# An FNet block with a feed-forward layer, in split float32 products: roots by GpSimd's power, first tiles of x rounded from x, the norms of the second half at other places

## The chip, the cores and the metric

The kernel runs on one core of a Trainium2 chip. A core has five engines, each with its own queue of instructions that it works through in order: TensorE (PE in the profile, with its weight loads as PEld), VectorE (DVE), ScalarE (ACT), GpSimd (POOL) and SyncE (SP), which here only issues transfers. The metric is the time of one execution on the device, in microseconds (us). The profile is one execution, recorded instruction by instruction; its span runs from the first to the last recorded instruction.

## The reference

```python
def reference(A_x, A_dft_seq_re, A_dft_seq_im, A_dft_hid_re, A_dft_hid_im, B_x, B_w1, B_w2):
    ...
        a = jnp.einsum("bsd,ed->bse", x, dft_hid_re)
        b = jnp.einsum("bsd,ed->bse", x, dft_hid_im)
        y = jnp.einsum("ts,bse->bte", dft_seq_re, a) - jnp.einsum("ts,bse->bte", dft_seq_im, b)
    ...
        h = jnp.einsum("bsd,df->bsf", x, w1)
        h = _silu(h)
        out = jnp.einsum("bsf,fd->bsd", h, w2)
    ...
    x = A_x
    h = x + _A_ref(_layernorm(x, axis=-1), A_dft_seq_re, A_dft_seq_im, A_dft_hid_re, A_dft_hid_im)
    h2 = h + _B_ref(_layernorm(h, axis=-1), B_w1, B_w2)
    return h2
```

x has 2048 rows of 512 columns, the hidden width is 1792, everything is float32. Both layer norms need the root 1 / sqrt(variance + 1e-5): one per row.

## The kernel before

**Split products.** Each float32 operand is split in two parts: a high part, rounded by ScalarE to a format that TensorE takes at full rate, and the remainder, subtracted by DVE. `three` (lines 108 to 112) multiplies high by high, high by remainder and remainder by high, so there are three matmuls for each product of a 128 x 128 and a 128 x 512 block. `rounded` (lines 74 to 85) makes the two parts of a page; in the profile they are `ph` (ACT, line 77) and `pl` (DVE, line 81). Many products are saved with a seven-product scheme (`fast`, `up`, `down_fast`), for which DVE makes sums and differences first.

**Stages.** Of the sequence, the even blocks of 512 positions are half q = 0 and the odd ones q = 1. The order of stages is `plain(0, 0)` (cosine part for half 0: 16 steps of 24 matmuls over four groups jj of four row tiles of x), `fast(1, 0)`, `mix(0)` (hidden transform and the sum with x, giving h), `fast(0, 1)`, `fast(1, 1)`, `mix(1)`, then `up(0)`, `down(0)`, `up(1)` and `down_fast(1)` for the feed-forward layer.

**Order.** Nothing is scheduled by a tool: `step(n, mm, before, after)` advances a clock by n matmuls of 0.2265 us, and puts work of other engines into a list of events at times relative to it (`before`: so many us ahead of the step; `after`: behind its end). At the end of the kernel the events are sorted by time and emitted, and ORDERED engines (PE, DVE, ACT, GpSimd) keep that order. The transfers on SP follow as they are emitted. So an event's time decides only where an instruction stands in its engine's queue; when it runs is decided by what it waits for.

**The head.** `begin` (line 230) issues the loads of the first two tiles of x and of the first two pages of the cosine matrix. For each of the two tiles `begin_x` (line 246) runs: `stats_x` (mean and variance per row, DVE lines 148 and 149), `roots_x` (line 152), then ScalarE rounds the page of the matrix and `norm_x` (line 160) writes the normalised tile `xc` (line 166) and from it the two high parts `X` (line 177); the remainders come from `rest` on DVE (line 183). The third and fourth tile (jj 0, k 1) follow in one go, events at lines 274 to 276. For jj 1 to 3 the four tiles' statistics go together into one call of `roots_x` with four columns (line 291).

**The root.** `rsqrt(v, t, r, q)` (lines 92 to 106), all on DVE: a first guess from the bits of v (lines 94, 95), the half of v (line 98), and three Newton steps, each of three instructions on more than one column and of two on one column.

**The norm of h** is `norm_h(q, tau, start)` (line 474), called four times. Its parts stand at fixed distances from `start`: load h again from memory (-8), column sums over the 512 values, which lie across partitions: two sums on DVE and an all-reduce over partitions on GpSimd (`total`, line 466; 0), subtract the mean (7, 9), squares on ScalarE (10, 12), the same sums and all-reduce for the variance (15), its 512 numbers through memory into a tile of 128 x 4 (22), the root on DVE and its way through memory to all partitions (31), and the products (45, 47). The transfers of h to memory and of these small tiles are issued by GpSimd too.

**The up projection**, `up(q, lead, between)` (line 600): for each of seven pairs p of column blocks, seven products n of six matmuls each, in the order 1, 2, 3, 6, 4, 7, 5 with 3 and 4 belonging to the pair before. They go into two tiles of PSUM, `y` and `vx`; DVE adds (line 624) and ScalarE copies and takes silu (lines 621 to 638). PSUM holds four such tiles, so the tiles of a pair are those of the pair two before, and a product waits for the adds that still read them.

```python
        for d, f in ((-8, load), (0, mean), (7, lambda: center(0)), (9, lambda: center(1)),
                     (10, lambda: square(0)), (12, lambda: square(1)), (15, var), (22, once),
                     (31, root), (45, lambda: scale(0)), (47, lambda: scale(1))):
            at(start + d, f)
```

```python
    second = down(0), down_fast(1)
    norm_h(1, 0, clock[0] + 8)
    norm_h(1, 1, clock[0] + 36)
    up(0, 28, lambda: next(second[0]))
```

Of the kernel before, what the change touches and what calls it, by code (L numbers as in the profile page):

```python
# [7 lines left out]
F32 = mybir.dt.float32  # L8
# [30 lines left out]
def fnet_ffn_kernel(  # L39
# [52 lines left out]
    def rsqrt(v, t, r, q):  # L92

        nc.vector.tensor_scalar(t.bitcast(I32), v.bitcast(I32), 1, None, op0=ALU.logical_shift_right)
        nc.vector.tensor_scalar(
            r.bitcast(I32), t.bitcast(I32), -1.0, float(0x5F3759DF), op0=ALU.mult, op1=ALU.add
        )
        nc.vector.tensor_scalar(v, v, -0.5, None, op0=ALU.mult)
        for a, b in ((r, q), (q, r), (r, q)):
            if a.shape[-1] == 1:  # L100
                nc.vector.scalar_tensor_tensor(t, a, v, a, op0=ALU.mult, op1=ALU.mult)
# [3 lines left out]
            nc.vector.scalar_tensor_tensor(b, t, 1.5, a, op0=ALU.add, op1=ALU.mult)  # L105
        return q
# [19 lines left out]
    def at(t, f):  # L126
        events.append((t, 1, len(events), f))
# [13 lines left out]
    def stats_x(jj, which):  # L141

        if jj not in stats:
            stats[jj] = [], small.tile([P, 4, 2], F32, name="mv1"), small.tile([P, 5, 4], F32, name="rs1")
        done, mv, _ = stats[jj]
        for k, a in which:
            st = small.tile([P, 6], F32, name="st1")
            nc.vector.bn_stats(st, xraw[jj, k][:, a, :])
            nc.vector.bn_aggr(mv[:, len(done), :], st)
            done.append((k, a))  # L150

    def roots_x(jj):
        done, mv, w = stats.pop(jj)
        n = len(done)
        nc.vector.tensor_scalar(w[:, 0, :n], mv[:, :n, 1], EPS, None, op0=ALU.add)
        r = rsqrt(*(w[:, m, :n] for m in range(4)))
        nc.vector.scalar_tensor_tensor(w[:, 4, :n], mv[:, :n, 0], -1.0, r, op0=ALU.mult, op1=ALU.mult)
        return {t: (w[:, 4, j : j + 1], r[:, j : j + 1]) for j, t in enumerate(done)}

    def norm_x(jj, which, factors):  # L160

        for k, a in which:
            if (jj, k) not in xc:
                xc[jj, k] = page(f"xc{jj}{k}")
            bias, scale = factors[k, a]
            nc.scalar.activation(xc[jj, k][:, a, :], xraw[jj, k][:, a, :], AF.Identity, bias=bias, scale=scale)
        todo = []
        for k in sorted({k for k, _ in which}):
# [4 lines left out]
            for i in range(2):  # L173
                if (i, k, jj) not in X:
                    X[i, k, jj] = page(f"X{i}{k}{jj}", F32R, (2, 2, 256))
                t, src = X[i, k, jj], xc[jj, k][:, b, i * 256 : (i + 1) * 256]
                nc.scalar.activation(t[:, 0, b], src, AF.Copy)  # L177
                todo.append((t[:, 1, b], src, t[:, 0, b]))
        return todo
# [66 lines left out]
    def begin_x(key, a):  # L246
        stats_x(0, [(0, a)])
        late["x", a] = begin_half(key, a) + norm_x(0, [(0, a)], roots_x(0))

    def plain(c, q):  # L250


        def mul(jj, k, tau, tiles, parts):
# [4 lines left out]
            for a in tiles:  # L258
                for i in range(2):
                    w = X[i, k, jj]  # L260
                    for m in range(2):
                        d = slice(m * P, (m + 1) * P)
                        three(acc[c, q, i, tau][:, m, :], w[:, 0, a, d], w[:, 1, a, d], hi[:, a, :], lo[:, a, :],
                              jj == 0 and k == 0 and a == 0, jj == NJ - 1 and k == 1 and a == 1)
# [3 lines left out]
        for a in range(2):  # L268
            at(-98 + 4 * a, lambda a=a: begin_x(keys[0], a))
            at(-97 + 4 * a, lambda a=a: rest(late.pop(("x", a))))  # L270
# [4 lines left out]
        at(clock[0] - 6, lambda: early("x0", lambda: norm_x(0, [(1, 0), (1, 1)], late.pop("r0"))))  # L275
        at(clock[0] - 4, lambda: rest(late.pop("x0")))
        for jj, k, tau in [(jj, k, tau) for jj in range(NJ) for k in range(2) for tau in range(2)][2:]:
# [4 lines left out]
            if k == 0 and tau == 0:  # L282
# [8 lines left out]
                before.append((15 - 5 * (jj == 1), lambda jj=jj: early(("r", jj), lambda: roots_x(jj))))  # L291
            if jj == NJ - 1 and k == 1:
# [181 lines left out]
    def norm_h(q, tau, start):  # L474
# [26 lines left out]
        def once():  # L501
            nc.gpsimd.dma_start(token[0], ln.pop("v")[0:1, 1, :])
            ln["w"] = small.tile([P, 4, 4], F32, name="rs2")
            nc.gpsimd.dma_start(ln["w"][:, 0, :], token[0].rearrange("(p j) -> p j", j=4))

        def root():
            w = ln.pop("w")
            nc.vector.tensor_scalar(w[:, 0, :], w[:, 0, :], 1.0 / D, EPS, op0=ALU.mult, op1=ALU.add)
            r = rsqrt(*(w[:, n, :] for n in range(4)))
            nc.gpsimd.dma_start(token[1].rearrange("(p j) -> p j", j=4), r)  # L510
# [352 lines left out]
    norm_h(1, 0, clock[0] + 8)  # L863
    norm_h(1, 1, clock[0] + 36)
# [6 lines left out]
    nc.vector.memset(warm, 0.0)  # L871
    nc.scalar.activation(small.tile([P, 1], F32, name="table"), warm[:, :1], AF.Silu)
# [49 lines left out]
```

## Time and profile before

| | us |
|---|---|
| median of 3 runs | 703.69 |
| the three runs | 703.64, 703.69, 704.99 |
| the profiled execution | 704.96 |
| its span | 703.2 |
| TensorE busy in it | 689.8 |
| DVE busy | 525.6 |
| ACT busy | 320.1 |
| GpSimd busy | 72.2 |

The page of the profile gives busy times and 40 slices of the span; the views of the trace give waits (who waited for whom), the instructions in order of time, and the chain of work that ended last, followed back from the end. A row of the timeline reads: start, duration, engine, line, operation, what it writes <- what it reads with the shapes, how many of them, and in square brackets how long the engine was idle before it and what ended that. The matmuls of the profile overlap, so that a step of 0.227 us from one start to the next is full rate, though each of them shows 0.39. Names such as `raw`, `ph`, `xc` are those of the code without their numbers. Instructions that only set up, wait or issue are not counted as busy.

### The profile page before, as it was taken

The page shows a single profiled execution, that of the slowest core. Times are in us where ns is not written, and L with a number is a line of the kernel's source. Part 1 is how long each engine was busy: PE and PEld are TensorE (multiplying, and loading weights), DVE is VectorE, ACT ScalarE, POOL GpSimd, SP SyncE. Part 2 cuts the span into 40 slices and gives each one's busy share as a digit, 9 for nine tenths or more (in the row PEclk, how much of TensorE's full clock was granted, in tenths as well). Part 3 has the DMA queues.
Part 4 walks back from the last instruction along what each step waited for, and adds up shares of the span by engine and source line. Part 5 has one row for each costly group of instructions (what it writes and reads, how often), then busy time and mean ns, then how long its engine had stood idle before and what let it go on. Part 6 is the DMA issues. An engine that isn't in the chain of part 4 may idle for free.

```text
span 703.2 us, 8359 instructions
## 1 busy us (share of the span) xinstructions
PE 689.8 (98%) x3009; PEld 565.4 (80%) x3009; DVE 525.6 (75%) x702; ACT 320.1 (46%) x398; POOL 72.2 (10%) x90
## 2 busy tenths in 40 slices
PE   8899999999999999999999999997999999999996
PEld 5688888888888888888888888886888888888885
DVE  6699965997867799799979746597888143249975
ACT  4555564444333644444363226565464044565420
POOL 0000020000013200022000003332320000000000
PEclk9999999999999999999999999999999999999999
DMA  9715359557779868687795664315997096368432
GB/s 324 277 57 180 114 206 382 196 203 239 231 233 377 339 217 311 246 298 280 271 330 181 194 232 153 103 46 209 372 411 309 10 337 229 120 245 294 135 135 89
DMA packets 54137, 160.22 MB, mean 228 GB/s; under 512 B 5968, under 2 KB 13136, under 8 KB 54096
## 3 DMA queue, kind: packets, MB, share of 16 engines
q1 hardware_dynamic: 44464, 126.11, 51.3%
q0 software_dynamic: 9632, 33.58, 12.2%
q8 instruction: 23, 0.38, 0.2%
q14 instruction: 18, 0.15, 0.1%
HBM read 122.95 MB, written 36.72 MB: 227 GB/s over the span
## 4 chain that ended last, share of the span: by engine, by line
PE 91%; DVE 4%; ACT 2%; issue 1%; DMA 0%; ACTq 0%; DVEq 0%
PE m L110 11%; PE m L111 11%; PE m L112 11%; PE y L110 7%; PE y L111 7%; PE y L112 7%; PE c L110 4%; PE c L111 4%; PE c L112 4%; PE o L110 4%; PE o L112 4%; PE o L111 4%; PE f L110 3%; PE f L112 3%; PE f L111 3%; PE vx L110 2%
## 5 line engine op out<-in xcount | busy, mean ns | idle before, releaser
L77 ACT ACTIVATE ph<-raw 128x1024 fp32r<-128x1024 f32 x98 | 101.8, 1058 | 98.1 <-DVE raw L356 62.2
L81 DVE TENSOR_TENSOR pl<-raw,ph 128x1024 fp32r<-128x1024 f32 x98 | 122.5, 1261 | 25.4 <-ACT ph L77 11.3
L110 PE MATMUL m<-ph,S 128*128 128x512 f32 x192 | 74.7, 389 | 0.0
L111 PE MATMUL m<-pl,S 128*128 128x512 f32 x192 | 74.7, 389 | 0.0
L112 PE MATMUL m<-ph,S 128*128 128x512 f32 x192 | 74.7, 389 | 0.0
L356 DVE TENSOR_TENSOR raw<-raw,raw 128x1024 f32<-128x1024 f32 x48 | 60.6, 1262 | 4.0 <-DMA raw<-in_seq 4.0
L110 PE MATMUL m<-ph,X 128*128 128x512 f32 x144 | 56.0, 389 | 0.0
L111 PE MATMUL m<-pl,X 128*128 128x512 f32 x144 | 56.0, 389 | 0.0
L112 PE MATMUL m<-ph,X 128*128 128x512 f32 x144 | 56.0, 389 | 0.0
L110 PE MATMUL c<-ph,X 128*128 128x512 f32 x128 | 50.0, 397 | 3.1 <-ACT X L177 3.1
L111 PE MATMUL c<-pl,X 128*128 128x512 f32 x128 | 50.1, 395 | 0.0
L112 PE MATMUL c<-ph,X 128*128 128x512 f32 x128 | 50.0, 395 | 0.0
L624 DVE TENSOR_TENSOR g<-vx,cp 128x512 f32<-128x512 f32 x28 | 19.2, 689 | 38.8 <-PE vx L112 30.9
L112 PEld LDWEIGHTS m<-ph,S 128*128 128x128 f32 x192 | 36.0, 188 | 7.5
L110 PEld LDWEIGHTS m<-ph,S 128*128 128x128 f32 x192 | 36.0, 188 | 7.5
L111 PEld LDWEIGHTS m<-pl,S 128*128 128x128 f32 x192 | 36.0, 188 | 7.4
L621 ACT ACTIVATE g<-g 128x512 f32<-128x512 f32 x42 | 26.4, 628 | 22.4 <-DVE g L624 22.4
L110 PE MATMUL o<-ph,Uh 128*128 128x512 f32 x84 | 33.5, 399 | 2.1 <-ACT g L621 2.1
L110 PE MATMUL f<-gth,wf 128*128 128x512 f32 x84 | 32.9, 392 | 0.8 <-DVE r L789 0.8
L112 PE MATMUL o<-ph,Ul 128*128 128x512 f32 x84 | 33.3, 397 | 0.0
L111 PE MATMUL o<-pl,Uh 128*128 128x512 f32 x84 | 33.3, 396 | 0.0
L111 PE MATMUL f<-gtl,wf 128*128 128x512 f32 x84 | 32.7, 389 | 0.0
(260 smaller groups left out, 1554.2 us busy)
## 6 DMA issues: line engine op xcount, KB each, us to landing
raw<-in_seq SPq DMA_DIRECT2D x98, 512.0 KB, 5.8
sf<-sd SPq DMA_DIRECT2D x28, 512.0 KB, 6.6
wf<-wd SPq DMA_DIRECT2D x28, 512.0 KB, 4.7
w<-in_ffn SPq DMA_DIRECT2D x28, 256.0 KB, 4.7
hid<-in_hid SPq DMA_DIRECT2D x8, 512.0 KB, 4.5
c<-cd SPq DMA_DIRECT2D x8, 512.0 KB, 4.6
h<-in_xT SPq DMA_DIRECT2D x8, 512.0 KB, 5.7
hd<-h POOLq DMA_DIRECT2D x8, 512.0 KB, 6.9
```

The lines of the kernel that those rows point to most:

```text
L77: nc.scalar.activation(hi, src, AF.Copy, scale=sign)
L81: nc.vector.tensor_tensor(lo, src, hi, op=ALU.subtract)
L110: nc.tensor.matmul(acc, wh, mh, start=first, stop=False, skip_group_check=on)
L111: nc.tensor.matmul(acc, wh, ml, start=False, stop=False, skip_group_check=on)
L112: nc.tensor.matmul(acc, wl, mh, start=False, stop=last, skip_group_check=on)
L356: nc.vector.tensor_tensor(o, a, b, op=ALU.subtract)
L621: nc.scalar.activation(g[q, f][:, tau, :], src, AF.Silu)
L624: nc.vector.tensor_tensor(g[q, f][:, tau, :], src, other, op=ALU.add)
```

## The change

1. `rsqrt` no longer computes the guess and three Newton steps on DVE. GpSimd raises v to the power -0.5 (exponents in a small tile `power`, filled once), and one Newton step on DVE refines the result. The Newton step is a function of its own, called later: in `norm_h` 1.5 us behind in the order (`spread`, with the transfers that follow), for jj 1 to 3 of x 2 us (1.5 for jj 1) behind, and in the head behind the remainder of the first page.
2. The tiles of group jj 0 are normalised with `direct=True`: ScalarE writes the two high parts straight from x with the norm's scale and bias, tile by tile, then `xc`; the remainders are still `xc` less the high part.
3. In `mul` of `plain`, the steps with jj 0 and tau 0 issue for each tile first the eight products with the high part of X, then the four with its remainder.
4. `norm_h(1, 0)` starts at -4 in place of 8 and `norm_h(1, 1)` at 16 in place of 36, from the end of `mix(1)`.

```diff
@@ -89,21 +89,22 @@
-    def rsqrt(v, t, r, q):
-
-        nc.vector.tensor_scalar(t.bitcast(I32), v.bitcast(I32), 1, None, op0=ALU.logical_shift_right)
-        nc.vector.tensor_scalar(
-            r.bitcast(I32), t.bitcast(I32), -1.0, float(0x5F3759DF), op0=ALU.mult, op1=ALU.add
-        )
-        nc.vector.tensor_scalar(v, v, -0.5, None, op0=ALU.mult)
-        for a, b in ((r, q), (q, r), (r, q)):
-            if a.shape[-1] == 1:
-                nc.vector.scalar_tensor_tensor(t, a, v, a, op0=ALU.mult, op1=ALU.mult)
+    power = keep.tile([P, 4], F32, name="power")
+
+    def rsqrt(v, t, q):
+
+        nc.gpsimd.tensor_tensor(q, v, power[:, : q.shape[-1]], op=ALU.pow)
+        nc.vector.tensor_scalar(t, v, -0.5, None, op0=ALU.mult)
+
+        def refine():
+            if q.shape[-1] == 1:
+                nc.vector.scalar_tensor_tensor(t, q, t, q, op0=ALU.mult, op1=ALU.mult)
             else:
-                nc.vector.tensor_tensor(t, a, a, op=ALU.mult)
+                nc.vector.tensor_tensor(v, q, q, op=ALU.mult)
                 nc.vector.tensor_tensor(t, t, v, op=ALU.mult)
-            nc.vector.scalar_tensor_tensor(b, t, 1.5, a, op0=ALU.add, op1=ALU.mult)
-        return q
+            nc.vector.scalar_tensor_tensor(q, t, 1.5, q, op0=ALU.add, op1=ALU.mult)
+
+        return refine
...
     def roots_x(jj):
+
         done, mv, w = stats.pop(jj)
         n = len(done)
...
+        v, t, r, b = (w[:, m, :n] for m in range(4))
+        nc.vector.tensor_scalar(v, mv[:, :n, 1], EPS, None, op0=ALU.add)
+        refine = rsqrt(v, t, r)
+
+        def then():
+            refine()
+            nc.vector.scalar_tensor_tensor(b, mv[:, :n, 0], -1.0, r, op0=ALU.mult, op1=ALU.mult)
+            return {x: (b[:, j : j + 1], r[:, j : j + 1]) for j, x in enumerate(done)}
+
+        return then
...
+        for k, a in which if direct else ():
+            for i in range(2):
+                put(X[i, k, jj][:, 0, a], k, a, slice(i * 256, (i + 1) * 256))
+            put(xc[jj, k][:, a, :], k, a, slice(0, 512))
+            todo += [(X[i, k, jj][:, 1, a], xc[jj, k][:, a, i * 256 : (i + 1) * 256], X[i, k, jj][:, 0, a]) for i in range(2)]
...
     def begin_x(key, a):
         stats_x(0, [(0, a)])
-        late["x", a] = begin_half(key, a) + norm_x(0, [(0, a)], roots_x(0))
+        then = roots_x(0)
+        rest(begin_half(key, a))
+        rest(norm_x(0, [(0, a)], then(), True))
...
+                if jj == 0 and tau == 0:
+                    for o, wh, _, mh, ml in todo:
+                        nc.tensor.matmul(o, wh, mh, start=first, stop=False)
+                        nc.tensor.matmul(o, wh, ml, start=False, stop=False)
+                    for o, _, wl, mh, _ in todo:
+                        nc.tensor.matmul(o, wl, mh, start=False, stop=last)
+                else:
+                    for v in todo:
+                        three(*v, first, last)
...
-        at(clock[0] - 6, lambda: early("x0", lambda: norm_x(0, [(1, 0), (1, 1)], late.pop("r0"))))
+        at(clock[0] - 6, lambda: early("x0", lambda: norm_x(0, [(1, 0), (1, 1)], late.pop("r0")(), True)))
...
                 before.append((15 - 5 * (jj == 1), lambda jj=jj: early(("r", jj), lambda: roots_x(jj))))
+                before.append((13 - 5 * (jj == 1) + 0.5 * (jj == 1), lambda jj=jj: early(("r", jj), late["r", jj])))
...
         def root():
+            w = ln["w"]
+            nc.vector.tensor_scalar(w[:, 0, :], w[:, 0, :], 1.0 / D, EPS, op0=ALU.mult, op1=ALU.add)
+            ln["q"] = rsqrt(*(w[:, n, :] for n in range(3)))
+
+        def spread():
             w = ln.pop("w")
...
+            ln.pop("q")()
+            nc.gpsimd.dma_start(token[1].rearrange("(p j) -> p j", j=4), w[:, 2, :])
             ln["r"] = page(f"r{q}{tau}")
             nc.gpsimd.dma_start(ln["r"][:, 0, :], token[1].partition_broadcast(P))
...
-                     (31, root), (45, lambda: scale(0)), (47, lambda: scale(1))):
+                     (31, root), (32.5, spread), (45, lambda: scale(0)), (47, lambda: scale(1))):
...
-    norm_h(1, 0, clock[0] + 8)
-    norm_h(1, 1, clock[0] + 36)
+    norm_h(1, 0, clock[0] - 4)
+    norm_h(1, 1, clock[0] + 16)
...
     nc.vector.memset(warm, 0.0)
+    nc.gpsimd.memset(power, -0.5)
```

More of the change, by code (lines that the diff above doesn't have):

```diff
@@ L154, in roots_x, with norm_x, put @@
         n = len(done)
[L155 to L162, printed above, removed]
+        v, t, r, b = (w[:, m, :n] for m in range(4))
[6 more added lines that the diff above has]
+        return then
+    def norm_x(jj, which, factors, direct=False):
+        for k in sorted({k for k, _ in which}):
             if (jj, k) not in xc:
                 xc[jj, k] = page(f"xc{jj}{k}")
+            for i in range(2):
+                if (i, k, jj) not in X:
+                    X[i, k, jj] = page(f"X{i}{k}{jj}", F32R, (2, 2, 256))
+        def put(o, k, a, e):
             bias, scale = factors[k, a]
-            nc.scalar.activation(xc[jj, k][:, a, :], xraw[jj, k][:, a, :], AF.Identity, bias=bias, scale=scale)
+            nc.scalar.activation(o, xraw[jj, k][:, a, e], AF.Identity, bias=bias, scale=scale)
         todo = []
+        for k, a in which if direct else ():
+            for i in range(2):
+                put(X[i, k, jj][:, 0, a], k, a, slice(i * 256, (i + 1) * 256))
+            put(xc[jj, k][:, a, :], k, a, slice(0, 512))
+            todo += [(X[i, k, jj][:, 1, a], xc[jj, k][:, a, i * 256 : (i + 1) * 256], X[i, k, jj][:, 0, a]) for i in range(2)]
+        if not direct:
+            for k, a in which:
+                put(xc[jj, k][:, a, :], k, a, slice(0, 512))
         for k in sorted({k for k, _ in which}):
@@ L172, in norm_x @@
                 xraw.pop((jj, k))
-            for i in range(2):
-                if (i, k, jj) not in X:
-                    X[i, k, jj] = page(f"X{i}{k}{jj}", F32R, (2, 2, 256))
+            for i in range(0 if direct else 2):
                 t, src = X[i, k, jj], xc[jj, k][:, b, i * 256 : (i + 1) * 256]
@@ L258, in mul @@
             for a in tiles:
+                todo = []
                 for i in range(2):
```

12 lines of the change are left out of this document (4 added, 8 removed).

## The prediction

> **What bounds the kernel now.** I read the page first, then the waits of TensorE, then the order of time around each wait. From the page:
>
> ```profile
> span 703.2 us, 8359 instructions
> PE 689.8 (98%) x3009; PEld 565.4 (80%) x3009; DVE 525.6 (75%) x702; ACT 320.1 (46%) x398; POOL 72.2 (10%) x90
> DMA  9715359557779868687795664315997096368432
> ```
>
> TensorE is busy for 98% of the span. The change removes none of its 3009 matmuls, so it can win only where TensorE waits. The DMA line will matter too: slice 0 (the first 17.6 us) is at 9 tenths, slices 24 to 26 (422 to 475 us) at 4, 3 and 1. The waits of TensorE (total, times, longest):
>
> ```profile
> PE c L110 <- ACT X L177: 3.1, 2, 2.0
> PE o L110 <- ACT g L621: 2.1, 1, 2.1
> PE vx L110 <- DVE g L624: 1.6, 1, 1.6
> ```
>
> So there are three places: the head, and two near the end of the up projection of half 0. The timeline of the head (start, duration, idle before):
>
> ```profile
> 0.33 0.10 POOL L915 MEMSET const-uint8-127<- 128x1 uint8 x1
> 0.72 1.28 ACT L872 ACT_TABLE_LOAD   x1 [0.72 <-PEq L915]
> ...
> 4.42 0.15 DVE L94 TENSOR_SCALAR rs<-rs 128x1 int32<-128x1 int32 x1
> ...
> 5.75 0.22 DVE L101 SCALAR_TENSOR_TENSOR rs<-rs 128x1 f32<-128x1 f32 x1
> ...
> 6.39 0.81 ACT L166 ACTIVATE xc<-x,rs 128x512 f32<-128x512 f32 x1 [1.83 <-DVE rs L157]
> 7.24 0.72 ACT L177 ACTIVATE X<-xc 128x256 fp32r<-128x256 f32 x2
> 7.71 0.80 PE L110 MATMUL c<-ph,X 128*128 128x512 f32 x2 [1.10 <-ACT X L177]
> ...
> 9.12 0.69 DVE L148 BATCH_NORM_STATS2 st<-x 128x6 f32<-128x512 f32 x1
> ...
> 13.52 0.76 DVE L183 TENSOR_TENSOR X<-xc,X 128x256 fp32r<-128x256 f32 x2 [0.72 <-ACT X L177]
> ...
> 14.35 0.69 DVE L183 TENSOR_TENSOR pl<-raw,ph 128x512 fp32r<-128x512 f32 x1
> ...
> 18.95 1.23 DVE L81 TENSOR_TENSOR pl<-raw,ph 128x1024 fp32r<-128x1024 f32 x1
> ...
> 21.29 0.50 PE L110 MATMUL c<-ph,X 128*128 128x512 f32 x1 [1.99 <-ACT X L177]
> ```
>
> The first product starts at 7.71, behind statistics, a root of 1.9 us (4.42 to 6.36) and two passes of ScalarE. The third tile of X comes at 21.29, after 2 us of idling. What that idling costs beyond itself stands in the chain that ended last:
>
> ```profile
> 23.03 0.43 PE c L111
> ...
> 28.24 0.23 PE c L111
> ```
>
> Nine matmuls after the wait step at 0.43 instead of 0.23 us, 1.8 us more. So the third tile really costs TensorE as much as an undisturbed arrival at 21.29 + 1.8 = 23.1. That is the mark of the head.
>
> **The change: roots.** A root of four columns loses eight small DVE steps of 0.2 us (12 before, 4 left), one of a single column six. DVE saves 1.2 to 1.6 us per call in ten calls. Most of that lies in stretches where DVE is ahead of TensorE and is worth nothing there. What comes in is one power on GpSimd and a hand-over each way. Less visible in the diff, and plain in the instruction order of the built kernel: GpSimd needs another code library for the power than for the all-reduce, so nine library reloads stand in its queue where one stood. They stand ahead of the very first power, then alternately ahead of an all-reduce and ahead of the power of each of the four norms of h (the second norm of half 1 pays two in a row).
>
> No row shows a reload's length. Bounds:
>
> ```profile
> 221.77 4.06 POOL L471 PARTITION_ALL_REDUCE m<-m  x1 [11.79 <-PE m L111]
> ```
>
> The only reload of the old kernel lies in the 11.79 us before the first all-reduce, which waited for its sums and then took 0.8 longer than the shortest (3.23, below). So a reload, R below, is between 0 and 11.8, or 12.6 if that 0.8 is part of it. Code has to come from memory, so the nearest rows are transfers; the load of a function table (1.28, above) is the nearest on the low side.
>
> ```profile
> raw<-in_seq SPq DMA_DIRECT2D x98, 512.0 KB, 5.8
> sf<-sd SPq DMA_DIRECT2D x28, 512.0 KB, 6.6
> x<-in_x SPq DMA_DIRECT2D x7, 512.0 KB, 8.5
> ```
>
> The last number is issue to landing, median. I take 8.5 in the crowded head (the x loads) and 6.6 in the up projection (sf, loaded there). For the power itself the ends are 0.10 (the memset) and 4.06 (an all-reduce of 128 times more elements). I take 0.5, close to the memset since it has one to four elements per lane.
>
> The Trainium skill (GPSIMD Engine Reference, section 2.1, Instruction dispatch) says that the first call to a freshly loaded kernel pays about 6 us, measured 5.95, with no visible profile instruction. The trace agrees so far as nothing is visible and 5.95 lies inside the bounds. By that figure at every place the formulas below give 703.7 - 1.7 + 0.6 = 702.6, no change that can be told; the rival of the short transfer is its nearest case.
>
> **Head.** GpSimd reaches its reload at 0.43 + 0.1 (memset of the exponents), after a barrier, so at about 0.75. The first power ends at 0.75 + R + 0.5, or at 4.9 if R is short. Two refinement steps and the bias take 0.64 (5.75 to 6.39). X is now rounded from x itself: one pass of 256 columns, 0.40 plus 0.07, replaces the 1.32 from 6.39 to 7.71. So the first product starts at 0.75 + R + 0.5 + 0.05 + 0.64 + 0.47 = R + 2.4, that is 10.9 with R 8.5, against 7.71.
>
> From there DVE and ScalarE set the third tile. Second tile: three passes of ScalarE (0.40, 0.40, 0.82), two remainders of X 0.76, pl 0.69, statistics 0.69, pl 0.69, two small steps 0.4, power 0.55, refinement 0.64: 6.0 after the first X began. Third: 1.62, 0.76, 0.69, statistics of two tiles 1.4, three small steps 0.6, then a large pl (1.23, which covers the power) and four small steps, 0.8: 7.0. Together 13.0 after the first product: R + 15.4, against the mark of 23.1, so **R - 7.7**. TensorE idles over 4 us before its first product and will be slow for the next nine matmuls, but it waits for DVE afterwards anyway, which covers that. With 8.5: **+0.8**. With R under 3.6 the gain ends at about -3.7, since the pl that now stands ahead of the refinement ends at 5.3. That products with the high part of X go first costs no matmul and lets the remainders arrive 1.6 us later.
>
> **Later roots and half 0.** In steps 1 to 3 the refinement stands 2 us behind its power with a pl of 1.2 between; the 1.6 us saved cover the rest. First norm of h:
>
> ```profile
> 245.50 0.59 POOL L504 DMA_DIRECT2D rs<-tk  x1 [4.29 <-DMA tk<-v]
> ...
> 257.24 0.39 PE L111 MATMUL m<-pl,S 128*128 128x512 f32 x1
> ```
>
> The reload follows the issue at 246.1; power and refinement end at 246.1 + R + 1.1, and the large pl after them (1.2, as at 18.95) must end by 257.24. That holds up to R = 8.8: nothing. Above, each us costs one.
>
> **The norms of half 1**, 12 and 20 us earlier. Their loads, on SP, now stand ahead of the weights of the up projection's second pair and wait for h to be stored; those weights are read only behind the rest of the mix and the 42 matmuls of the first pair (9.5 us at 0.227): nothing. On GpSimd the first all-reduce goes ahead of two stores of h, which DVE does not have ready before it ends: nothing. Gain first:
>
> ```profile
> 468.99 3.03 DVE L517 TENSOR_TENSOR hr<-hr,r 128x512 f32<-128x512 f32 x2
> ...
> 477.37 1.28 DVE L624 TENSOR_TENSOR g<-vx,cp 128x512 f32<-128x512 f32 x2
> ```
>
> L517 ran beside an all-reduce and took 3.0 instead of 1.3; this and the sums of the second norm made the add late that frees the bank. They go, and with them the wait of vx: **-1.6**. The wait at 488.65 does not go. Its chain is
>
> ```profile
> 483.67 0.34 DVE v L683
> ...
> 485.17 1.06 ACT Uh L77
> ...
> 488.65 0.50 PE o L110
> ```
>
> and has nothing of the norms in it; the removed root stood behind it.
>
> What is late next is the second norm's root, behind three reloads:
>
> ```profile
> 428.57 0.69 DVE L624 TENSOR_TENSOR g<-vx,cp 128x512 f32<-128x512 f32 x1 [2.15 <-PE vx L112]
> ...
> 425.12 3.81 POOL L471 PARTITION_ALL_REDUCE m<-m  x1 [8.09 <-DVE m L470]
> ...
> 441.33 0.50 POOL L502 DMA_DIRECT2D tk<-v  x1 [0.29 <-POOL v L471]
> 443.68 0.59 POOL L504 DMA_DIRECT2D rs<-tk  x1 [1.84 <-DMA tk<-v]
> ...
> 459.57 0.56 POOL L510 DMA_DIRECT2D tk<-rs  x1 [2.09 <-DVE rs L105]
> 463.94 0.55 POOL L512 DMA_DIRECT2D r<-tk  x1 [3.81 <-ACT g L621]
> 468.64 3.23 POOL L471 PARTITION_ALL_REDUCE v<-v  x1 [4.14 <-ACT Uh L77]
> ```
>
> DVE has the second mean's sums ready near 432 (behind the add of 428.6, with two contended sums). All-reduce 3.8: 435.9. Store and fetch of the first variance 0.3 + 2.35 + 0.6: 439.1. Reload 6.6, power 0.5, refinement 0.6: 446.8. L510 to L512 and its issue 4.4 + 0.55: 451.8. Reload 6.6: 458.4. All-reduce 3.2 and 0.3 + 2.35 + 0.6: 464.8. The root's input lands 3.8 after its issue, as the store of L510 did before L512 (4.4 less 0.55): 468.0. Last reload, power, refinement: 472.5. DVE is in order: behind its wait for the input stands an add (0.7, so 468.7) that TensorE's V product needs; behind its wait for the power stand four sums (1.5) and the add (0.7) that frees the bank pair for the next pair's X product, so 474.7.
>
> ```profile
> 466.45 0.39 PE L110 MATMUL vx<-T7h,sf 128*128 128x512 f32 x1
> ...
> 470.53 0.39 PE L110 MATMUL vx<-T2h,wah 128*128 128x512 f32 x1
> ```
>
> TensorE would be there at 466.45 and 470.53: 2.2 us and, all counted, 4.2 us late. If the first wait brings slow matmuls they fill part of the second. Three reloads lie in the sum, so **max(0, 4.2 + 3 (R - 6.6)) - 1.6**, +2.6 with 6.6.
>
> **Sum.** +0.8 + 2.6 = +3.4 on the profiled span of 703.2. That execution took 704.96, so 1.8 lie around the span, and is 1.3 above the median of the three runs, 703.69. A difference carries over: 707.1. Differences under 0.2% (1.4 us) can't be told from none with this kernel.
>
> **The rivals.** (1) A reload costs what the commonest transfer costs, 5.8, everywhere. For it: 98 such rows; against: the head is crowded. Head -1.9, norms 1.8 - 1.6: 702.0, barely faster; with one R in both places the change breaks even at 6.2. (2) Reloads are short like the table load, or do nothing where the library is resident from the run before. Head -3.7, norms -1.6: 698.4. (3) Reloads of 9 everywhere: +1.3 in the head, 0.2 in half 0, 11.4 - 1.6 in half 1: 714.7; at the bound of 11.8 some 729. Against: DMA is nearly idle from 440 to 475. If the wait of vx stays though its norm has moved, the forecast's own case ends 1.6 higher.
>
> **Chances.** Forecast 0.45 (own range 704 to 711), rival 1 0.25, rival 2 0.14, rival 3 0.16. Faster: rival 2 and half of rival 1, 0.27. Same: the other half and the lower edge of the forecast, 0.17. Slower 0.56. The range, 699.5 to 715, leaves out most of rival 2 and the upper half of rival 3, under 0.2.
>
> **What would show it.** First power on GpSimd: ends near 9.8 (forecast), 7.1 (rival 1), 5 (rival 2). First product: 10.9, 8.2, 6.6. The wait at the third X under 1 us with no 0.43 steps after it. Around 463 to 474, DVE waiting twice for rs, with TensorE's vx waiting for the add behind. The wait of o for g unchanged. The prediction is wrong if GpSimd's queue shows the powers ready when DVE asks for them, or if TensorE waits for something else than roots.

## The result and the profile after

The changed kernel takes 710.47 us, the median of six executions (707.28, 711.06, 710.23, 710.71, 710.16, 712.3), against 703.63 for the kernel before, measured with it (six, 702.04 to 704.99). The ratio is 1.0095, 95% interval 1.007 to 1.012: slower by 6.8 us. The prediction, 707.1 in a range of 699.5 to 715, has the sign and its range holds the time, but its sum is 3.4 us short, and its terms did not come out as they stand there. The profiled execution is the quickest of the six, 707.28 with a span of 705.5. A second set of executions of the same kernel (e10) gave 710.97, ratio 1.0104 (1.0075 to 1.0132), with a profiled span of 708.6.

The page of the changed kernel, span, engines and the chain that ended last:

```profile
span 705.5 us, 8331 instructions
...
PE 689.4 (98%) x3009; PEld 563.7 (80%) x3009; DVE 513.1 (73%) x628; ACT 321.4 (46%) x400; POOL 83.9 (12%) x101
...
PE 86%; DMA 5%; DVE 3%; issue 2%; ACT 1%; POOL 1%; SPq 0%; DVEq 0%; POOLq 0%; ACTq 0%
```

VectorE lost 74 instructions and 12.5 us of work, as the change promises, and the kernel got longer: TensorE's share of the last chain fell from 91 to 86%, so more of the end is set by waits. TensorE's waits (total, times, longest):

```profile
PE vx L111 <- DVE g L660: 4.1, 2, 3.7
PE o L111 <- ACT g L657: 2.0, 1, 2.0
PE m L112 <- DVE pl L81: 1.3, 2, 1.1
PE c L290 <- ACT X L179: 1.3, 2, 1.1
...
PE c L111 <- ACT X L197: 0.4, 1, 0.4
```

The waits of the head are down from 3.1 to 1.7, the wait of o is what it was, m waits for pl (half 0, new), and vx waits 3.7 at one stroke where it had waited 1.6.

Three rows cut the execution into stretches with the same work in both kernels: a store of wS2h behind the head, the first store of h behind the norms of half 0, and the end. Before (GpSimd's timeline):

```profile
162.07 0.53 POOL L579 DMA_DIRECT2D sd<-wS2h  x1 [57.77 <-ACT wS2h L77]
...
392.24 0.53 POOL L425 DMA_DIRECT2D hd<-h  x1 [36.67 <-DVE h L421]
```

After (GpSimd's timeline, with the powers and the steps around the second norm of half 1):

```profile
0.73 0.10 POOL L908 MEMSET power<- 128x4 f32 x1 [0.29 <-POOLq L952]
4.73 0.57 POOL L96 TENSOR_TENSOR rs<-rs,power 128x1 f32<-128x1 f32 x1 [3.90 <-DVE rs L158]
...
159.72 0.53 POOL L615 DMA_DIRECT2D sd<-wS2h  x1 [57.77 <-ACT wS2h L77]
...
243.93 0.59 POOL L536 DMA_DIRECT2D rs<-tk  x1 [4.64 <-DMA tk<-v]
252.41 1.05 POOL L96 TENSOR_TENSOR rs<-rs,power 128x4 f32<-128x4 f32 x1 [7.89 <-issue]
...
340.90 1.05 POOL L96 TENSOR_TENSOR rs<-rs,power 128x4 f32<-128x4 f32 x1 [9.48 <-issue]
...
391.83 0.53 POOL L457 DMA_DIRECT2D hd<-h  x1 [33.55 <-DVE h L453]
...
444.32 1.05 POOL L96 TENSOR_TENSOR rs<-rs,power 128x4 f32<-128x4 f32 x1 [7.05 <-issue]
...
449.50 0.56 POOL L548 DMA_DIRECT2D r<-tk  x1 [2.50 <-DMA tk<-rs]
456.26 3.25 POOL L503 PARTITION_ALL_REDUCE v<-v  x1 [6.20 <-ACT cp L672]
459.80 0.71 POOL L534 DMA_DIRECT2D tk<-v  x1 [0.29 <-POOL v L503]
461.86 0.59 POOL L536 DMA_DIRECT2D rs<-tk  x1 [1.34 <-DMA tk<-v]
470.21 1.05 POOL L96 TENSOR_TENSOR rs<-rs,power 128x4 f32<-128x4 f32 x1 [7.76 <-issue]
```

The head gained 2.35 (162.07 to 159.72). From there to the store of h it took 232.11 instead of 230.17, a loss of 1.94 in half 0. From the store of h to the end of the span it took 313.67 instead of 310.96, a loss of 2.71. Together +2.3, 703.2 to 705.5.

The first power waited for its input from VectorE (L158) and for nothing else: no reload there. The four powers of the norms stood 7.05 to 9.48 us behind the instruction before them; "issue" means that they waited for nothing that the profile shows. That is the reload. The view of the power's line counts both kinds:

```profile
L96 POOLq MODIFY_POOL_CONFIG  x10: 11/37/42, 1.0 to 462.5; - x10
L96 POOL TENSOR_TENSOR rs<-rs,power x10: 545/1054/2035, 4.7 to 470.2; 128x4 f32<-128x4 f32 x7, 128x1 f32<-128x1 f32 x2, 128x2 f32<-128x2 f32 x1
...
  DVE rs L158: 55.4, 6
  issue: 32.2, 4
...
  DVE rs L103: 17.2, 7
```

The first row is GpSimd's queue: pairs of short records, one pair ahead of the first power and one at the start of each of the four long stretches. Four more pairs stand at the all-reduces; the kernel before has a single pair, at its first all-reduce. These are the places that the prediction names, and e3 and e4 below show that the stretches go when the power does. Six powers waited for their input from VectorE, four for 32.2 us in all (8.05 each) on the reload, and VectorE, which works in order, stood idle for 17.2 us in seven waits for powers. What that does to TensorE (its timeline, from the third X of the head on):

```profile
19.51 0.50 PE L290 MATMUL c<-ph,X 128*128 128x512 f32 x1 [1.12 <-ACT X L179]
...
255.26 0.50 PE L112 MATMUL m<-pl,S 128*128 128x512 f32 x1 [0.20 <-DVE pl L81]
...
343.74 0.50 PE L112 MATMUL m<-pl,S 128*128 128x512 f32 x1 [1.13 <-DVE pl L81]
...
473.98 0.79 PE L111 MATMUL vx<-T2h,wah 128*128 128x512 f32 x1 [3.70 <-DVE g L660]
474.57 0.63 PE L112 MATMUL vx<-T2l,wah 128*128 128x512 f32 x1
...
477.36 0.50 PE L111 MATMUL y<-T3h,sf 128*128 128x512 f32 x1 [0.46 <-ACT cq L674]
...
482.09 0.50 PE L111 MATMUL vx<-T7h,sf 128*128 128x512 f32 x1 [0.36 <-DVE g L660]
```

and VectorE ahead of the long wait:

```profile
463.79 0.17 DVE L540 TENSOR_SCALAR rs<-rs 128x4 f32<-128x4 f32 x1 [2.10 <-DMA rs<-tk]
463.99 0.17 DVE L97 TENSOR_SCALAR rs<-rs 128x4 f32<-128x4 f32 x1
464.17 0.69 DVE L660 TENSOR_TENSOR g<-vx,cp 128x512 f32<-128x512 f32 x1
471.30 0.16 DVE L103 TENSOR_TENSOR rs<-rs 128x4 f32<-128x4 f32 x1 [6.44 <-POOL rs L96]
...
473.25 0.68 DVE L660 TENSOR_TENSOR g<-vx,cp 128x512 f32<-128x512 f32 x1
```

The power's input was there at 463.96 and the power came at 470.21. VectorE idled 6.44 us for it, with four sums and the add at 473.25 behind, and TensorE's vx waited for that add.

### The profile page after: what moved, and what is told of

Its sections match the earlier page's. It is cut to its first block, busy times and chain, and to the rows that moved or that the text cites. A ratio compares the mean times of both kernels' runs of the same rounds, so it can differ in the third digit from the quotient of the medians.

```text
span 705.5 us, 8331 instructions
## 1 busy us (share of the span) xinstructions
PE 689.4 (98%) x3009; PEld 563.7 (80%) x3009; DVE 513.1 (73%) x628; ACT 321.4 (46%) x400; POOL 83.9 (12%) x101
## 3 DMA queue, kind: packets, MB, share of 16 engines
q0 software_dynamic: 9632, 33.58, 12.5%
## 4 chain that ended last, share of the span: by engine, by line
PE 86%; DMA 5%; DVE 3%; issue 2%; ACT 1%; POOL 1%; SPq 0%; DVEq 0%; POOLq 0%; ACTq 0%
PE m L112 9%; PE m L113 9%; PE m L111 9%; PE y L113 7%; PE y L112 7%; PE y L111 7%; PE o L111 4%; PE o L113 3%; PE o L112 3%; DMA raw<-in_seq 3%; PE f L111 3%; PE f L113 3%; PE f L112 3%; PE c L111 3%; PE c L113 3%; PE c L112 3%
## 5 line engine op out<-in xcount | busy, mean ns | idle before, releaser
L81 DVE TENSOR_TENSOR pl<-raw,ph 128x1024 fp32r<-128x1024 f32 x98 | 120.6, 1241 | 24.5 <-ACT ph L77 14.9
L111 PE MATMUL c<-ph,X 128*128 128x512 f32 x112 | 43.4, 391 | 0.4 <-ACT X L197 0.4
L112 PE MATMUL c<-pl,X 128*128 128x512 f32 x112 | 43.7, 390 | 0.0
L113 PE MATMUL c<-ph,X 128*128 128x512 f32 x112 | 43.6, 389 | 0.0
L657 ACT ACTIVATE g<-g 128x512 f32<-128x512 f32 x42 | 26.3, 627 | 19.4 <-DVE g L660 19.4
L111 PE MATMUL f<-gth,wf 128*128 128x512 f32 x84 | 32.9, 392 | 0.8 <-DVE r L825 0.8
L77 ACT ACTIVATE gth<-g 128x1024 fp32r<-128x1024 f32 x21 | 22.1, 1058 | 23.3 <-DVE g L813 20.7
L113 PE MATMUL f<-gth,wf 128*128 128x512 f32 x84 | 32.7, 389 | 0.0
```

What stands on the lines that cost most here:

```text
L77: nc.scalar.activation(hi, src, AF.Copy, scale=sign)
L81: nc.vector.tensor_tensor(lo, src, hi, op=ALU.subtract)
L111: nc.tensor.matmul(acc, wh, mh, start=first, stop=False, skip_group_check=on)
L112: nc.tensor.matmul(acc, wh, ml, start=False, stop=False, skip_group_check=on)
L113: nc.tensor.matmul(acc, wl, mh, start=False, stop=last, skip_group_check=on)
L657: nc.scalar.activation(g[q, f][:, tau, :], src, AF.Silu)
```

## The experiments

Ten runs, in three groups on the same chip within each. Each row of the table gives the time beside the kernel before of its group (703.56 to 703.79), and the three stretches of its profiled execution, found by the same rows as above, as a difference to the kernel before (162.07; 230.17; 310.96).

| kernel | median us | ratio (95%) | head | half 0 | rest |
|---|---|---|---|---|---|
| changed kernel | 710.47 | 1.0095 (1.007-1.012) | -2.35 | +1.94 | +2.71 |
| e1: all-reduce last | 714.12 | 1.0139 (1.0117-1.0161) | +2.59 | +1.29 | +6.32 |
| e2: power in h alone | 713.97 | 1.0139 (1.0114-1.0164) | +1.26 | +4.41 | +6.43 |
| e3: no power | 703.17 | 0.9988 (0.9976-1.000) | +1.39 | 0.00 | -2.29 |
| e4: power in x alone | 704.37 | 1.0001 (0.999-1.0011) | +2.36 | -0.01 | -2.35 |
| e5: old places | 711.01 | 1.0103 (1.0088-1.0119) | -2.31 | +2.40 | +5.41 |
| e6: places alone | 700.46 | 0.9953 (0.9935-0.9972) | +0.08 | 0.00 | -2.28 |
| e7: direct rounding alone | 704.66 | 1.001 (1.0001-1.002) | +1.24 | 0.00 | -1.64 |
| e8: power in x, one more last | 700.71 | 0.9946 (0.9932-0.9959) | -2.28 | 0.00 | -3.92 |
| e9: e8 without direct rounding | 700.38 | 0.9944 (0.9927-0.996) | -2.57 | +0.60 | -2.33 |
| e10: changed kernel again | 710.97 | 1.0104 (1.0075-1.0132) | -2.29 | +1.72 | +5.97 |

One thing has to be known to read the columns: a wait of TensorE of about 2 us is followed by seven or eight matmuls at 0.43 us in some executions and in others not, 1.6 to 1.7 us each time. The kernel before has two such waits (21.29 and 488.65), and its executions lie in three groups, near 702.0, 703.5 and 705.1, with granted clocks of 0.998, 0.996 and 0.994. The profile of before has both; those of the changed kernel, e1, e5, e7 and e8 have none behind the wait of o, so 1.6 of their last column is that. The head column holds the same thing: behind the third X only the profiles of before and e6 have such steps, and e1 and e4 have them behind their first product. Beside an execution of before without them the gains in the head are smaller and the losses larger. An estimate: the executions of before near 702.0 have a span of 700.2; less 230.17 for half 0 and 309.32 for the rest (310.96 less 1.64, as in e7), their head ends near 160.7. Against that the changed kernel, e8 and e9 gain about 1.0 in the head, and e2, e3 and e7 lose 2.6 to 2.8.

**e1. What the start finds.** The changed kernel, and one all-reduce on GpSimd behind its last store:

```diff
+    def leave():
+        end = keep.tile([P, 2, 4], F32, name="end")
+        nc.gpsimd.memset(end[:, 0, :], 0.0)
+        nc.gpsimd.partition_all_reduce(end[:, 1, :], end[:, 0, :], channels=P, reduce_op=REDUCE_ADD)
+
+    at(1e6, leave)
```

> One all-reduce of four zeros is added on GpSimd behind its last store, where nothing waits for it (GpSimd is idle from 531 us on in the changed kernel). Theory A: GpSimd has to fetch the code of the power again after an all-reduce (6 to 8 us), and what it ran last in one execution is still there in the next; so the profiled execution of the changed kernel (707.3, first power at 4.7) began without a fetch and its five others (709 to 712) with one. Then the first power here ends between 8.5 and 11 in every execution, the first product starts between 9.5 and 11.5 instead of 6.7, the span is 708 to 710 and the times 709.5 to 711.5, ratio 1.008 to 1.012. Theory B: the start never fetches, and the executions of the changed kernel differ by something in the norms. Then the first power is at 4.7 again, the first product at 6.7, and the times are 707 to 711 as spread as before.

The first power (GpSimd's timeline) and the first product (TensorE's):

```profile
9.65 0.59 POOL L96 TENSOR_TENSOR rs<-rs,power 128x1 f32<-128x1 f32 x1 [8.83 <-issue]
```

```profile
11.57 0.79 PE L290 MATMUL c<-ph,X 128*128 128x512 f32 x1 [4.02 <-ACT X L179]
```

An instruction at the very end moved the first power from 4.73 to 9.65 and the head from -2.35 to +2.59. So what GpSimd ran last is still there when the next execution begins, and the changed kernel, whose last such function is a power, starts without a reload. On that point theory A holds. Its other half fell: I had put the spread of the changed kernel's executions down to the start, and expected 709.5 to 711.5 here; it is 714.12, 3.7 above the median of the changed kernel, which a kernel that always reloads should only have matched. So the other executions of the changed kernel probably start without a reload too, and lose their extra time further on. That is argued and not shown for each of them; e10 shows one.

**e2. Power in the norms alone.** The roots for x have the old chain on VectorE back; the rest is as changed.

```diff
-        v, t, r, b = (w[:, m, :n] for m in range(4))
+        v, t, s, r, b = (w[:, m, :n] for m in range(5))
         nc.vector.tensor_scalar(v, mv[:, :n, 1], EPS, None, op0=ALU.add)
-        refine = rsqrt(v, t, r)
+        root_v(v, t, s, r)
```

(root_v is the rsqrt of the kernel before; the call of refine goes too.)

> The roots for x are computed on VectorE again (shift, subtraction and three Newton steps); the power stays in the four norms of h, and the direct rounding and the places of the norms stay as changed. Theory A: the head has no power, so it no longer depends on what ran before: the third X is ready near 19.7, the head gains about 2.3 in every execution, the norms lose what they lose in the profiled execution of the changed kernel (about 4.8 from 37 us to the end), and all executions lie within 1.5 us of each other around 706.5 (ratio 1.004). Theory B: the times spread as those of the changed kernel, 707 to 711, median 709 or more.

713.97: a miss on two counts. The head did not keep its gain (+1.26), so the gain was the power's and not the direct rounding's. And half 0 lost 4.41, by one reload, the longest of all (GpSimd's timeline, then TensorE's):

```profile
345.39 1.05 POOL L96 TENSOR_TENSOR rs<-rs,power 128x4 f32<-128x4 f32 x1 [12.68 <-issue]
```

```profile
348.22 0.62 PE L128 MATMUL m<-pl,S 128*128 128x512 f32 x1 [2.51 <-DVE pl L81]
```

**e3. No power.** As e2, and the norms of h as in the kernel before, at their changed places.

```diff
-            ln["q"] = rsqrt(*(w[:, n, :] for n in range(3)))
+            r = root_v(*(w[:, n, :] for n in range(4)))
```

> Both roots are computed on VectorE as in the kernel before; the direct rounding, the order of products in the head and the places of the norms stay as changed. Theory A: all the loss is the power's code fetches. The head gains about 2.3, the wait of vx near 478 goes (1.6), nothing else moves: 699.5 to 700.5, ratio 0.995. Rival C: the moved norms are themselves a loss, since their all-reduces and sums now run beside the first pairs: 702 to 705, with a wait of vx for g between 425 and 475.

Half 0 is back to 0.00 and the rest turns into a gain of 2.29, so the powers in the four norms cost all that was lost there: between e2 and e3 10.8 us in the medians, between e1 and e4, which differ in the same edit and the last all-reduce, 9.75. The time, 703.17, lies above the 699.5 to 700.5 expected, because of the head: I expected -2.3 and it is +1.39. VectorE's timeline there:

```profile
5.27 0.69 DVE L201 TENSOR_TENSOR pl<-raw,ph 128x512 fp32r<-128x512 f32 x1 [0.17 <-ACT ph L261]
...
8.99 0.76 DVE L201 TENSOR_TENSOR X<-xc,X 128x256 fp32r<-128x256 f32 x2 [1.87 <-ACT xc L177]
```

The new order puts a pl of 0.69 into the middle of the old root's chain. And the remainder of X now waits 1.87 us for ScalarE, since xc is written behind both halves of X; before it waited 0.72. With the old root VectorE is what the head hangs on: the third X comes at 22.72 instead of 21.29, and at 35.16 TensorE waits 0.94 for the X of the next group (L195).

**e4. Power in x alone.** The edit of e3 in the norms without that of e2 in x: the norms of h have their old root at the changed places; the last GpSimd function of an execution is then an all-reduce.

> The power stays in the roots for x; the four norms of h have the roots of the kernel before, on VectorE, at their changed places. The last GpSimd function of an execution is then an all-reduce. Theory A: each execution starts with a fetch, so the first power ends between 8.5 and 11, the first product starts at 9.5 to 11.5, and the time is that of the kernel without any power plus 3 to 4.5: 703 to 704.5, ratio 0.999 to 1.001. Theory B (no fetch at the start): 699.5 to 700.5, first product at 6.7.

704.37, as expected: the first power starts at 9.45, the first product at 11.37, the head ends 2.36 later, half 0 loses nothing, the places gain 2.35.

**e5, e6, e7. The other two parts.** e5 is the changed kernel with the norms at 8 and 36; e6 is the kernel before with only the two places changed; e7 is e3 with the places at 8 and 36. The edit shown is that of e6; e5 and e7 take it back.

```diff
-    norm_h(1, 0, clock[0] + 8)
-    norm_h(1, 1, clock[0] + 36)
+    norm_h(1, 0, clock[0] - 4)
+    norm_h(1, 1, clock[0] + 16)
```

> The changed kernel with the two norms of the second half at their old places (8 and 36 instead of -4 and 16). Theory A (a root behind a code fetch costs wherever it stands, since VectorE waits for it in order): still slower than the kernel before by about as much or more, 709 to 716. Rival D (the loss comes from the close places, where the two norms' powers and all-reduces alternate): the loss of the norms mostly goes, 702 to 706.

> The kernel before with nothing changed but the places of the two norms of the second half (-4 and 16 instead of 8 and 36); all roots on VectorE, no power. Theory A: the wait of vx near 478 and the short one before it go, 1.7 to 2.0 less: 701.5 to 702.0, ratio 0.997 to 0.9975; the wait of o for g stays at 2.25. Rival: the places gain nothing by themselves (0.999 to 1.001).

> The kernel before with the direct rounding of the first tiles of x and the head's order of products and roots alone; all roots on VectorE, no power, norms at their old places. By the kernel without any power, whose head ended 1.2 later than that of before: 704.5 to 705.2, ratio 1.0012 to 1.002. Rival: the direct rounding helps by itself as the prediction's arithmetic has it, 1 to 2.5 less: 701 to 702.7.

e5, 711.01: with the powers the places give nothing that can be told (710.47 and 710.97 with them). VectorE there waits 9.00 us for one power at 465.81, and TensorE's vx 5.7. e6, 700.46: the places alone gain 3.3 us in the medians. In its profile the wait of vx is gone and the wait of o is not (TensorE's waits):

```profile
PE c L110 <- ACT X L177: 2.9, 2, 2.0
PE o L110 <- ACT g L621: 2.1, 1, 2.1
```

The profile gives 2.28; that the medians give 1 us more than this and the expectation I can only argue: three of its six executions lie at 699.6 to 699.7 with a clock of 0.998 to 0.999, so without any matmuls at 0.43, and of 17 of before in that group none. Beside the fastest executions of before in the other groups (702.0) those three gain 2.4, as the profile has it. e7, 704.66: direct rounding alone costs 0.9 us in the medians. Its profile has no matmuls at 0.43 behind any wait (704.54, clock 0.998), and beside the executions of before near 702.0 that is 2.5.

**e8. The start without a reload.** e4, and one power of four ones behind the last store:

```diff
+        end = keep.tile([P, 4], F32, name="end")
+        nc.gpsimd.memset(end, 1.0)
+        nc.gpsimd.tensor_tensor(end, end, power, op=ALU.pow)
```

> As the kernel with the power in the roots for x alone, and one more power, of four ones, on GpSimd behind its last store, where nothing waits for it, so that each execution leaves the power's code behind for the next. Theory A: the first power starts at 4.7 without a fetch, the first product at 6.7, the head ends 2.3 to 2.8 earlier than before, the moved norms give 1.9: 699 to 700, ratio 0.993 to 0.995. Rival (what an execution leaves behind doesn't matter, and the profiled execution of the changed kernel started early for another reason): as without the last power, 704.4, first product at 11.4.

```profile
4.80 0.56 POOL L96 TENSOR_TENSOR rs<-rs,power 128x1 f32<-128x1 f32 x1 [3.98 <-DVE rs L174]
```

700.71, and the first power at 4.80: e1 turned round. The head gains 2.28 where e4 lost 2.36, from an instruction that nothing waits for; the medians of the two are 3.7 apart. That an execution behind another program would pay the reload is to be expected, but no run shows it.

**e9. Is it the direct rounding?** e8, with the first tiles of x normalised and then copied, as before (the last argument of norm_x left out, here and for the third tile).

```diff
-        rest(norm_x(0, [(0, a)], then(), True))
+        rest(norm_x(0, [(0, a)], then()))
```

> As the kernel with the power in the roots for x and one more power at its end, but the first tiles of x are again normalised first and then copied into X. Theory A (direct rounding is worth what it saves on ScalarE where the root no longer holds VectorE): X of the third tile comes 1.5 later (two activations of 0.76 and a copy of 0.58 instead of one of 0.55), near 21.1, a wait of about 2.5 instead of 1.2, in some executions with slow matmuls behind it: 701.5 to 703.5, ratio 0.996 to 0.9995. Rival (the direct rounding gives nothing even then, since the residuals on VectorE come later with it): 700.0 to 701.0, ratio 0.994 to 0.996.

700.38: the rival holds. The head is 0.3 quicker without the direct rounding. Half 0 lost 0.60 in this profile, where m waited 0.31 for pl behind the first norm, though no norm of h has a power here; why was not followed up. e6, e8 and e9 are the quickest kernels of this study; their intervals overlap, so they are not ranked. So the times show no gain of the power in x beside the places alone, and e6 needs neither a power nor a start left by the execution before.

**e10. The changed kernel again.**

> The changed kernel unchanged, beside the others. If what ran last decides the start, its first power is at 4.7 again and the head ends 2.5 earlier than before; the fetches ahead of the four powers of h measure 7 to 13, the longest where the DMA is busiest (near 331 to 344), and the times lie at 709 to 712 by the length of that fetch. If not, the first power comes near 9.6.

The head is the same to 0.1 (first power 4.75, head -2.29). The difference of 3.1 in the span lies behind the store of h, and it begins with a small transfer (GpSimd's timeline, then TensorE's):

```profile
459.72 0.71 POOL L534 DMA_DIRECT2D tk<-v  x1 [0.29 <-POOL v L503]
463.69 0.59 POOL L536 DMA_DIRECT2D rs<-tk  x1 [3.25 <-DMA tk<-v]
471.75 1.05 POOL L96 TENSOR_TENSOR rs<-rs,power 128x4 f32<-128x4 f32 x1 [7.47 <-issue]
```

```profile
468.21 0.50 PE L111 MATMUL vx<-T7h,sf 128*128 128x512 f32 x1 [2.16 <-DVE g L660]
...
475.52 0.50 PE L111 MATMUL vx<-T2h,wah 128*128 128x512 f32 x1 [2.93 <-DVE g L660]
```

The store of the variance cost GpSimd 3.25 us of waiting instead of 1.34, and the root's input is late enough that VectorE stalls for it as well. TensorE then waits twice. e1 shows the same (3.54 us, and two waits of vx, 5.4 together). So executions differ by such a transfer, by what half 0 loses (1.94 in the first profile of the changed kernel, 1.72 here, 1.29 in e1, 4.41 in e2) and by the matmuls at 0.43. The loss of half 0 does not follow the length of its second reload alone, which was 9.48, 11.01, 10.12 and 12.68: here the reload began sooner, and the power came at 340.74 instead of 340.90. How much of the spread each makes over all executions of the changed kernel, two profiles of it can't tell.

## Why the prediction was right or wrong

**Powers and reloads.** That the powers bring reloads, where they stand, and that VectorE would stand in order behind them is what the profiles show. Of the signs it named, VectorE waits twice for rs between 463 and 474 (2.10 and 6.44 us) with vx behind, and the wait of o is unchanged; but the first power ended at 5.3, which was the sign of rival 2. R in the norms was taken as 6.6; in the profile after it is 7.05, 7.76 and 7.89 ahead of three of the powers, 9.48 ahead of the fourth, and 6.20 ahead of the all-reduce between two powers. The power itself, taken as 0.5, is 0.57 for one column and 1.05 for four. The Trainium skill (GPSIMD Engine Reference, section 2.1, Instruction dispatch) has about 6 us, measured 5.95: the reload ahead of the all-reduce agrees (6.20), those ahead of a power in the norms are 1.0 (6.97, e2) to 6.7 us (12.68, e2) longer.

**Head: wrong in a condition.** R = 8.5 was the right size where there is a reload: 8.83 in e1, 8.62 in e4, first product at 11.57 and 11.37 against a forecast of 10.9. Its reason, that a crowded DMA makes a reload long, is not shown (see the last section), so the size owes something to luck. But the step "ahead of the very first power" failed: in the changed kernel the library is there from the execution before. That is the second half of rival 2, which had been given 0.14 and was worked out for all places at once; it is true for the first reload and false for the others. By its floor the head should gain 3.7, with the third X at 19.4 (23.1 less 3.7), and it gained 2.35. The working up to the third X was right: it came at 19.51, and the 61st matmul, behind the slow steps of before, started 3.4 us sooner (22.38 against 25.80). What the sum left out stands behind it: TensorE lost 0.3 at 25.74, behind a pl (L81) that ended at 25.69, and 0.8 from 31.45 on, where it waited for the X of the four-column root (L197). With the reload the head loses 2.4 to 2.6 where the sum had +0.8; in e4 it is 1.25 at the 61st matmul, and the same 0.3 and 0.8 follow.

**What makes the head's gain.** The prediction gave the direct rounding the saving on ScalarE (1.32 to 0.47) for each tile. e3, e7 and e9 show that this part, with its order of the head, is a loss of 1.2 to 1.4 in the head with the old root (2.6 to 2.8 by the estimate above) and no gain with the power. With it the first product starts 0.7 sooner (6.73 in e8, 7.40 in e9), but the first remainder comes 0.5 later (7.92 against 7.38), VectorE takes its work in order, and the first tiles of the next group are normalised 1.55 later (29.28 against 27.73). The gain is the shorter root on VectorE, and of the 2.35 some 1.6 are the steps at 0.43 that followed the wait of 1.99 at the third X before and did not follow the 1.12 after.

**Half 0: nothing up to R 8.8, wrong.** The first norm's bound was a little too high: with R 7.89 TensorE already waits (255.26), since the power took 1.05 and not 0.5 and the trip before it 0.35 longer. The second norm was not worked out, and it is the one with the longest reload, 9.48 to 12.68. Cost 1.3 to 4.4. The waits of 0.20 and 1.13 make up the 1.94 of the profiled execution: TensorE fell back by 0.47 and 1.44 at them, about 0.3 more than it idled.

**Norms of half 1: right in the chain.** The gain is there as forecast: vx no longer waits for the old sums (e6), and the wait of o for g stays (2.0 after 2.1). The new chain came out close: the last power ends at 471.26, the add stands behind four sums, and vx waits 3.70 against 4.2 forecast. Errors cancel in it: the last R is 7.76 instead of 6.6 and the powers take 1.05 instead of 0.5, but the input landed 1.9 us after its issue instead of 3.8. Where the trip is longer, as in e10, the first wait comes too, 2.16 against 2.2 forecast. What the sum lacked is what follows a wait: the six matmuls from 473.98 to 477.36 took 3.38 us instead of 1.36 (steps of 0.43 to 0.59, then 0.46 for cq), and 482.09 brought another 0.36.

**Sum.** +3.4 was forecast on the profiled span; the profiled execution has +2.3, as -2.35 + 1.94 + 2.71. That the two lie close is luck: the head is 3.2 under its term, half 0 is 1.9 over, and the 2.71 for half 1, against +2.6, hold 1.6 of gain that is only the missing slow steps behind the wait of o. The median has +6.8. The profiled execution was the quickest of six, and the terms that vary (reload of half 0, transfer of the variance, what follows a wait) were forecast by single values from one execution of the kernel before, in which they do not matter. Two sums of the prediction are slightly off, which changes nothing: the terms of the third tile give 7.1 and not 7.0, and those of rival 3 give 715.0 and not 714.7.

## What to carry to other kernels

A function on GpSimd that needs another library than its neighbours (here the power beside the all-reduce) costs a reload at each change between them, and where an in-order engine waits for its result, the reload (6 to 13 us here) is in the chain; shortening the arithmetic by 1.5 us does not pay for it. Look at which function an execution leaves behind and which it asks for first: e4 and e8 differ by one power behind the last store, and their heads by 4.6 us in the profiles. And before a saving on one engine is counted, see whether the engine behind it takes its work in an order that gives the saving back.

## What the runs showed of the hardware

The longest reloads lie where there is much traffic, but traffic alone does not make them long. The windows of the changed kernel during three reloads (stretch, length, busy time and count of each engine, granted clock, DMA share, GB/s):

```profile
331.40:340.90 9.50, 9.50 (x44) 7.86 (x43) 5.65 (x7) 3.19 (x3) 0.02 (x1) 1.00 0.74 279
437.30:444.30 7.00, 7.00 (x33) 5.79 (x32) 3.72 (x7) 4.87 (x7) 0.00 (x0) 1.00 0.18 51
450.10:456.30 6.20, 6.20 (x30) 5.11 (x29) 3.52 (x5) 3.65 (x7) 0.04 (x1) 1.00 0.29 81
```

At a DMA share of 0.74 the power's reload took 9.5 us, at 0.18 7.0; the all-reduce's took 6.2 at 0.29. But the power's took 7.15 in e5 with no DMA at all beside it (457.57 to 464.72, share 0.00), at most 7.6 in e5 at 0.92 (484.91 to 492.50) and 7.22 behind the last store of e8 at 1.00 (522.94 to 530.16), and the all-reduce's took 5.80 behind the last store of e1 at 1.02 (539.30 to 545.10). So the share does not set it. The five longest, 9.48 to 12.68, are those of the second norm of half 0 in the five profiles that have a power there; what makes them long was not tried.

The steps at 0.43 us are stretches in which the granted clock is 0.50, 3.4 us long (22.36 to 25.78 in the profile of before) or twice that (10.62 to 17.45 in e1). The wait of o, 2.0 to 2.1 us idle in each of the twelve profiles, was followed by them in seven and not in five (the changed kernel, e1, e5, e7, e8). The wait of 2.51 for pl in e2 was followed by them; those of 2.5 us in the head of e3 and of e7 were not, nor that of 2.93 in e10. The Trainium skill (TensorE: Matmul & The Clock Gate, Part 1) has the clock fall after an idle window of about 3.4 us that runs freely, so that it varies from run to run: the variation agrees, but here a wait of 2 us was enough in seven of twelve cases.
